# First modulation weights over 128 partitions, and Q and K of token tiles 4 to 7 with the tokens stationary, in a transformer block with dilated local attention

## The chip, the core and the metric

The kernel runs on one core of a Trainium2 chip. A core has five engines that work side by side: TensorE (PE in the profile, its weight loads apart as PEld), VectorE (DVE), ScalarE (ACT), GpSimd (POOL) and SyncE (SP), which here only issues DMAs. Each engine takes its instructions in program order and waits on semaphores for the others. PE multiplies a stationary operand (loaded first, at most 128x128) with a moving one, and its sums go to PSUM, from where ACT or DVE copy them out; all other data lies in SBUF, 128 partitions wide. A DMA can also turn a tile (rows to columns) on its way from SBUF to SBUF; in the profile that is DMA_TRANSPOSE.

The metric is the device time of one execution in microseconds (us), the median of several runs.

## What is computed

```python
mod = (silu(c) @ w_mod).reshape(1, 6, 1, 448)        # c is 1 x 448, w_mod 448 x 2688
sa, ca, ga, sb, cb, gb = six rows of mod
h = layernorm(x) * (1 + ca) + sa                     # x is 1 x 2048 x 448
x = x + ga * attention(h, wqkv, wo)
h = layernorm(x) * (1 + cb) + sb
x = x + gb * mlp(h)          # layernorm, 448 -> 1792, tanh gelu, 1792 -> 448, with biases
```

The attention has 16 heads of 28 channels. Token s attends to the 8 tokens s, s-2, ..., s-14, as far as they exist. Inputs and the output are bf16.

## The kernel before

**Tokens.** Because of the step of 2, even and odd tokens never meet in the attention. A *token tile* p (0 to 7) holds 128 even and 128 odd tokens; the index `s` or `n` (0 or 1) tells them apart. 448 channels are three full rows of 128 and a half row of 64 (`KT = 4`, `KS = 64`).

**The head of the kernel.** `c` is laid out as columns by four small matmuls (`c_cols`), silu is made of it, and `silu_bc` holds it for use in matmuls. The first two sixths of `w_mod` (sa and ca) are loaded into `wm_st` as 112 partitions by 4 rows (`MW = 112`, `KM = 4`), in two DMAs of 588 and 196 KB. `mod_cols` (L396, 40 matmuls) turns them into the columns `mod_col`, which scale and shift the normalized tokens (`affine`, L475 and L477) into `hT`, channels on partitions. The other four sixths go through `wmod2` and `mods` (L597) to `mod_bc` by way of a small buffer in HBM (L604, L606).

**Q and K** (`front_qk`). The weights are staged in `wqk_st` and `wqr_st`, and `spread` (L418 to L427) copies them to `Wqk` and `Wqr` with 32 columns for each head's 28, so that a group of four heads fills 128 partitions. These 128 columns are the stationary operand, and up to 512 tokens move: the sum stands in PSUM with channels on partitions, as the attention wants it, and ACT copies it to `qT` or `kT`. Tiles 0 and 1 go alone, then 2 and 3, 4 and 5, 6 and 7 as pairs. A pair costs, for Q and K together, four groups of 6 matmuls with 128 rows (L526) and 4 with 64 rows (L532, two of which run side by side).

**Attention** in 9 batches of 114 positions: V from `hT` (`v0` to `v8`; batches 5 to 8 first copy overlapping windows of `hT` into `hw`, L646), logits (`lt`, L695), exp, mask, the sum of the weights (`pd`) and the weighted V (`po`, L728), whose product with the inverse sum (`omul`, L745) is written over `qT`. `out_proj` (`wo0` to `wo7`, L760) is followed by two layer norms on DVE, with the power -1/2 on POOL (L447); their result `zy` is turned to `yT` by DMA (L791). The first layer norm of tiles 4 to 7 is turned by DMA as well (`zT`, L500); that of tiles 0 to 3 by PE.

**MLP** by pairs of tiles: `w1` (L526 and L532 with `yT`), gelu on ACT, `w2` (L840), the residual and the store. It comes in three phases between which ACT changes its function table, and the later attention batches run between `w2` matmuls.

**What sets the order.** All work is first recorded as numbered tasks with an engine each. `emit` then issues them in the order of a table, `ORDER`: `n` is a task's number, `n:A`, `n:D`, `n:P` an engine other than its first choice (ACT, DVE, POOL), `n:R` a variant of a PE task with the half rows first, and `n+k@m` puts k *fillers* ahead, matmuls on zeros of 128x256 (L369) which keep PE at work while it waits. `SLOTS` picks for each temporary tile one of the buffers of its kind (`ROOM`); PSUM has four (`P`). So each engine's sequence is fixed; nothing is decided while it runs. SP issues all loads, turns and stores in one sequence, but for one small load by ACT.

Of the kernel before, what the change touches and what calls it, by code (L numbers as in the profile page):

```python
# [9 lines left out]
FP32 = mybir.dt.float32  # L10
BF16 = mybir.dt.bfloat16
ACT = mybir.ActivationFunctionType
ALU = mybir.AluOpType
# [4 lines left out]
KM, MW = 4, 112  # L18
# [5 lines left out]
LEAD = 8  # L24
PLACE = (0, 2, 1, 3)
WT = LEAD + SL + 8
# [10 lines left out]
UNITS = [[0], [1], [2, 3], [4, 5], [6, 7]]  # L37
PHASES = [(range(0, 5), [0]), (range(5, 7), [1]), (range(7, 9), [2, 3])]
ROOM = {"P": 4, "et": 2, "den": 2, "zy": 4, "h2": 3, "yT": 3, "hm": 2, "vb": 3, "xp": 3, "hw": 2}
# [10 lines left out]
]  # L50
ORDER = """
0 13 3 15 1 9 14 7 16 6 17 11 10 12 8 18 19 5 2 52+9@52 4 20 60 21 58 53 22 61 54 59 55 23 62 56 63 57 64 24 68+10@68
65 66 67 25 69 70 26 76 71 27 77 72 73 74 28 75 84+10@84 78 85 29 81 86 82:A 30 98 90+3@90 83:A 31 91 80:A 96 92 93
94:R 99 79 32 97 128 100 87 120 101 88:R 95 33 102 103 164 34 121 89 129 130 35 118 104:A 36 189 105 165 131 119 166
190 132 122 108 133 37 109:A 169 106 107:A 187 123 170 179 209+5@209 38 177 167 124 125 113 134 210 39 168 114:R 135
178 126 180 136:A 254 40 127 181 115 244 182 137 255 188 110 246 138:A 41 141 111:R 191 171 42 139:A 245 192 150 256
43 112 140 44 172 183 151 311 193 45 174 257 247 184 46 258 248 185 152 175 194 214 312:D 259 211 146 186 215 195 261
212 260 216 142:R 148 262:D 196 213 249 147 144:D 263 250 143:R 251 149 252:D 153 47 217 145 48 173 49 218 200 219 50
197 276 198 51 199:A 176 253 220 205 418 154 277 221 156 278 207 281 159 206 155 279 161 282 162 222 280 208 283 266:A
157 284 285 223 286 201 158 287 224 163 202:R 203 225 288 264 316 267 204 313 226 289 265 317 227 160 314 228 318 269  # L60
290 229 454:A 315 348 271 351 291 273 293 352 292 230 294 231 349 295 353 272:R 275 232 350 268 233 274 296 236 234
116 298 319 270 297 320 117 235 299 354 321 346 237 300 356 238 301 239 419 322 303 302 240 347 304 241 305 323 455:R
306 527:A 242:D 307 357 243 308 355 309:D 324 381 358 310 456 359 325 420 563:A 328 528 360 329 397:R 326 529 363 361
382 364 327 362 398 330 365 331 399 366 332 367 368 387:R 333 386 369 383 334 384 370 385 335 371 400 404 392 373 391
336 401 389 374 372 337 388 338 402 375 390 339 340 341 460 394 411 403 395 396 342 343 393 413 376 344:A 417 345 378
377 414 379 461 380 457 421 462 458 424 412 425 459 407 422 415 426 416 408 423 428 427 463 429 405 465 406 430 466
564 431 490 409 464 506 565 410 467 496:R 507 508 468 497 499 500 432 469 498 470 491 472 433 471 473 434 474 436 475
501:R 435 494 437 438 477 492 476 439 495 493 478 440 569 441 503 479 520 504 442 505 480 509 512 482 502 522 481 511
526 483 484 523 443 570 513 446 533 444 566 485 534 447 530 445 521 448 571 531 486 514 535 567 532 568 536 524 449
573 538 515 510 525 539 450 537 487 451 572 488:A 540 516 452 489 574 575 453 541 599 576 517 542 577 518 543 519 615  # L70
578 545 600:R 579 616 581 617 546 580 582 544 583 547 584 548 605 603 585 604 550 586 602 549 587 601 551 588 610:R
609 552 607 589 618 619 555 608 591 621 606 590 553 620 556 625 592 554 611 593 557 613 558 614 623 622 612 559 626
560 594 561:A 562 631 595 596 597:D 598 629 630 624 635 627 628 650:R 638 639 637 632 636 652 640 653 654 633 651 657
634 655 656 645:R 641 644 643 642 664 648 649 646 660 647 665 658 666 667 659 668 669 661 670 671 672 662 673 663 674
675
# [76 lines left out]
def kernel(  # L152
# [65 lines left out]
    c_row = cst.tile([1, D], BF16, name="c_row")  # L218
    one1 = cst.tile([1, 128], BF16, name="one1")
    zys = [cst.tile([128, NS, DP], BF16, name=f"zy{i}") for i in range(ROOM["zy"])]  # L220
    e_c = cst.tile([MW, KM], FP32, name="e_c")
    silu_bf = cst.tile([MW, KM], BF16, name="silu_bf")
    silu_bc = cst.tile([MW, KM, HP], BF16, name="silu_bc")
# [8 lines left out]
    wm_st = sb("hm", [MW, KM, 2 * D], BF16, "wm_st")  # L232
    wqk_st = sb("hm", [128, KT - 1, 2 * D + HP - DH], BF16, "wqk_st")
    wqr_st = sb("yT", [128, 2 * D + HP - DH], BF16, "wqr_st")
    wmod2 = sb("hm", [MW, KM, 4 * D], BF16, "wmod2")
# [81 lines left out]
    def load_rest(a):  # L317
        load(lambda a=a: nc.sync.dma_start(out=wqr_st.t[KS * a:KS * a + KS, :], in_=A_wqkv[(KT - 1) * 128:D, 0:2 * D + HP - DH]),
             0.36, [f"wr{a}"], bufs=[wqr_st])
# [11 lines left out]
    add("ACT", 0.4, lambda: nc.scalar.dma_start(out=c_row[:], in_=c), writes=["c"], late=1.8, name="load c")  # L331
    tbl0 = add("ACT", 1.28, lambda: nc.scalar.preload_act_table_set(EXP_SET), name="tbl")
    load_x(0, 1)
    KP = (range(KM - 1), range(KM - 1, KM))
# [13 lines left out]
    for k in range(KM):  # L348
        load(lambda k=k: nc.sync.dma_start(out=wmod2.t[:, k, :], in_=w_mod[k * MW:(k + 1) * MW, 2 * D:6 * D]), 1.5, [f"wmod2{k}"],
             bufs=[wmod2])  # L350
# [23 lines left out]
    def c_cols():  # L374
        for k in range(KM):
            nc.tensor.matmul(psc.t[0:MW, 0, 128 * k:128 * k + 128], lhsT=c_row[0:1, k * MW:(k + 1) * MW], rhs=one1[:], start=True, stop=True)

    add("PE", 0.45, c_cols, mode="32x128", reads=["c", "one1", "warm_w"], bufs=[psc], fills=[psc], name="c_cols")
    add("ACT", 0.12, lambda: nc.scalar.activation(out=e_c[:], in_=psc.t[0:MW, 0, 0:128 * KM:128], func=ACT.Exp, scale=-1.0), bufs=[psc],
# [3 lines left out]
    add("DVE", 0.08, lambda: nc.vector.tensor_tensor(out=silu_bf[:], in0=e_c[:], in1=psc.t[0:MW, 0, 0:128 * KM:128], op=ALU.mult),  # L383
        reads=["e_c"], bufs=[psc], writes=["silu"], name="silu")
    add("ACT", 0.3, lambda: nc.scalar.copy(out=silu_bc[:], in_=silu_bf[:].unsqueeze(2).to_broadcast([MW, KM, HP])),
# [3 lines left out]
    def mod_cols(i):  # L389
        for j in range(KT):  # L390
            for v in range(2):
                for kt in KP[i]:

                    for a in range(2 if j == KT - 1 else 1):
                        m = KS if j == KT - 1 else 128
                        nc.tensor.matmul(pscol[i].t[KS * a:KS * a + m, 0, (v * KT + j) * HP:(v * KT + j + 1) * HP],  # L396
                                         lhsT=wm_st.t[:, kt, v * D + j * 128:v * D + j * 128 + m], rhs=silu_bc[:, kt, :],
                                         start=(kt == KP[i][0]), stop=(kt == KP[i][-1]),
                                         tile_position=(0, KS * a) if j == KT - 1 else None)

    head_tr, head_norm = ([], []), ([], [])

    def modulation():
        for i in range(2):
            add("PE", (0.8, 0.32)[i], lambda i=i: mod_cols(i), reads=["silu_bc", f"wm{i}"], bufs=[pscol[i], wm_st], fills=[pscol[i]], mode="F>128x64",
                name="mod_cols", instr=(60, 20)[i], after=head_tr[i])
            part = add_col if i == 0 else mod_col
            add("DVE", 0.08, lambda i=i, part=part: nc.vector.tensor_tensor(out=mod_col[:], in0=pscol[i].t[:, 0, 0:2 * KT * HP:HP], in1=part[:], op=ALU.add),
                bufs=[pscol[i]], reads=["add_col"], writes=["sca"], after=head_norm[i], name="sca")
# [73 lines left out]
    def front_ln(u, on_act, dma=False):  # L483
# [5 lines left out]
        for q, p in enumerate(u):  # L489
# [20 lines left out]
            if p == 0:  # L510
                head_norm[0].append(P.tasks[-1])
            tr_task = add("PE", 0.45, tr, reads=["ident"] + zk, bufs=[*ptr, z], writes=[(ptr[0], q)], instr=16, name=f"tr{p}")
            if p == 0:
                head_tr[1].append(tr_task)
                modulation()
# [396 lines left out]
```

## Time and profile before

| | |
|---|---|
| runs | 176.03, 176.88 and 177.47 us, median 176.88 |
| span of the profiled execution, first to last instruction | 174.2 us |
| median less span | 2.7 us |
| granted TensorE clock, mean | 1.000 |
| PE matmuls | 2152 |
| HBM read and written | 9.81 MB and 1.84 MB |

The page names no time of the profiled execution beside its span. A span is measured from the first instruction to the last, so a constant part before and after is missing in it; the table gives what it comes to against the median.

In the profile's lists a group reads: line, engine, operation, tiles (out<-in), shapes, count, then busy us and mean ns of one, then the idle time just ahead of it and who ended it. For matmuls the mean is the time of one through the pipeline; the next one starts earlier, so the cost of a row of them is read from the chain of waits, where consecutive pieces are given from start to start.

### The profile page before, as it was taken

How to read it: one execution, taken by the hardware profiler on the slowest of the kernel's cores; microseconds unless marked ns; L12 is line 12 of the kernel's file. 1: busy time of each engine (PE TensorE's matmuls, PEld its weight loads, DVE VectorE, ACT ScalarE, POOL GpSimd, SP SyncE). 2: the span in 40 equal slices, each digit the busy share in tenths (PEclk: the TensorE clock that was granted, in tenths of full speed). 3: DMA queues.
4: the chain of work that ended last, by engine and by line, in shares of the span. 5: the costliest groups of instructions: out<-in, count | busy, mean ns of one | idle time of the engine just before them, and what ended most of it. 6: DMA issues, size and time to landing. Idle time of an engine off the chain costs nothing.

```text
span 174.2 us, 4984 instructions
## 1 busy us (share of the span) xinstructions
PE 167.4 (96%) x2152; PEld 84.9 (49%) x2152; DVE 115.1 (66%) x289; ACT 108.1 (62%) x147; POOL 42.5 (24%) x60
## 2 busy tenths in 40 slices
PE   7799999998999999999999999999899999999993
PEld 4585564353454444444555353554444455344562
DVE  6477998569999989796254259998597950220103
ACT  3156989497889798478939644976625840166400
POOL 6002134003013320367000004655003840053000
PEclk9999999999999999999999999999999999999999
DMA  5999999989000014000610100001910028100002
GB/s 146 294 307 297 237 212 338 221 235 229 6 0 4 4 30 93 4 0 0 124 56 0 56 0 0 4 0 56 124 53 0 2 45 79 55 36 17 0 30 79
DMA packets 20708, 15.12 MB, mean 87 GB/s; under 512 B 13705, under 2 KB 19726, under 8 KB 20686
## 3 DMA queue, kind: packets, MB, share of 16 engines
q1 hardware_dynamic: 20684, 14.80, 36.2%
q8 instruction: 17, 0.28, 0.7%
q14 instruction: 5, 0.04, 0.1%
q10 hardware_dynamic: 2, 0.00, 0.0%
HBM read 9.81 MB, written 1.84 MB: 67 GB/s over the span
## 4 chain that ended last, share of the span: by engine, by line
PE 83%; DVE 9%; DMA 3%; issue 1%; ACT 1%; SPq 0%
PE p L840 21%; PE p L526 18%; PE pq L526 12%; PE pw L760 6%; PE pv L663 5%; PE p L532 3%; DMA wm_st<-in_w_mod_dram 3%; PE po L728 3%; PE pv L526 3%; PE pq L532 3%; PE lt L695 3%; DVE stt L431 3%; DVE h L776 2%; DVE h L451 2%; PE pq L369 1%
## 5 line engine op out<-in xcount | busy, mean ns | idle before, releaser
L821 ACT ACTIVATE hm<-p,b_col 128x512 bf16<-128x512 f32 x56 | 34.1, 689 | 30.7 <-PE p L532 25.2
L840 PE MATMUL p<-w_s,hm 128*128 128x448 bf16 (+1 forms) x238 | 44.4, 342 | 0.6 <-issue 0.6
L526 PE MATMUL p<-yT,w_s 128*128 128x512 bf16 x168 | 38.5, 380 | 0.0
L447 POOL TENSOR_TENSOR rs_all<-tv_all,neg_half 128x2 f32<-128x2 f32 x22 | 18.2, 832 | 79.8 <-DVE tv_all L445 79.8
L840 PEld LDWEIGHTS <-hm 128*128 128x128 bf16 x238 | 22.7, 98 | 19.7 <-issue 1.4
L526 PEld LDWEIGHTS <-w_s 128*128 128x128 bf16 x168 | 15.7, 98 | 20.9 <-issue 3.4
L846 DVE TENSOR_TENSOR x_all<-p,x1p 128x896 bf16<-128x896 f32 (+2 forms) x10 | 9.0, 904 | 24.9 <-PE p L840 24.8
L526 PE MATMUL pq<-hT,Wqk 128*128 128x512 bf16 (+1 forms) x108 | 22.2, 345 | 0.0
L431 DVE BATCH_NORM_STATS2 stt<-x_all 128x6 f32<-128x448 bf16 x32 | 18.4, 610 | 0.2
L798 POOL TENSOR_TENSOR x1p<-x_all,gbb_bc 128x448 f32<-128x448 bf16 x16 | 17.6, 1122 | 0.0
L702 ACT ACTIVATE et<-lt 128x928 bf16<-128x928 f32 x18 | 16.0, 946 | 1.3 <-PE lt L695 1.3
L745 DVE TENSOR_TENSOR qT<-po,den 128x912 bf16<-128x912 f32 x9 | 9.9, 1103 | 7.0 <-ACT den L739 5.2
L526 PEld LDWEIGHTS <-Wqk 128*128 128x128 bf16 x108 | 9.4, 98 | 9.7 <-issue 2.9
L708 DVE TENSOR_TENSOR et<-et,mask 128x928 bf16<-128x928 bf16 x18 | 11.2, 644 | 3.6 <-ACT et L702 3.6
L760 PE MATMUL pw<-wo_s,qT 128*128 128x448 bf16 x64 | 13.1, 353 | 0.0
L767 DVE TENSOR_TENSOR x_all<-pw,x_all 128x896 bf16<-128x896 f32 x8 | 8.7, 1084 | 6.6 <-PE pw L760 6.6
L586 ACT CAST kT<-pq 128x1024 bf16<-128x1024 f32 x8 | 8.1, 1015 | 5.3 <-PE pq L532 3.3
L737 ACT ACTIVATE den<-pd 128x928 f32<-128x928 f32 x9 | 8.3, 946 | 4.6 <-PE pd L717 4.6
L776 DVE TENSOR_TENSOR h<-h,mod_bc 128x896 bf16<-128x896 bf16 x16 | 10.2, 672 | 0.0
L739 ACT ACTIVATE den<-den,den_bias 128x928 f32<-128x928 f32 x9 | 9.5, 1072 | 0.1
L431 DVE BATCH_NORM_STATS2 stt<-h 128x6 f32<-128x448 bf16 x16 | 9.1, 614 | 0.1
L760 PEld LDWEIGHTS <-qT 128*128 128x128 bf16 x64 | 6.0, 98 | 5.7 <-issue 0.2
(102 smaller groups left out, 184.0 us busy)
## 6 DMA issues: line engine op xcount, KB each, us to landing
wmod<-in_w_mod_dram SPq DMA_DIRECT2D x4, 392.0 KB, 10.5
w_s<-in_B_w_dram SPq DMA_DIRECT2D x7, 224.0 KB, 5.7
out_dram<-x_all SPq DMA_DIRECT2D x7, 224.0 KB, 2.6
x_all<-in_A_x_dram SPq DMA_DIRECT2D x3, 448.0 KB, 5.5
w_s<-in_B_w_dram SPq DMA_DIRECT2D x3, 448.0 KB, 4.8
wqk_st<-in_A_wqkv_dram SPq DMA_DIRECT2D x3, 225.0 KB
wm_st<-in_w_mod_dram SPq DMA_DIRECT2D x1, 588.0 KB, 5.8
x_all<-in_A_x_dram SPq DMA_DIRECT2D x2, 224.0 KB
```

The source lines that it names most:

```text
L431: add("DVE", 0.53, lambda: nc.vector.bn_stats(out=stt[:, w, b, :], in_=src()), reads=reads, bufs=bufs, after=early if w == b == 0 else (), ...
L447: add("POOL", 0.55 + 0.17 * n, lambda: nc.gpsimd.tensor_tensor(out=r, in0=tv, in1=neg_half[:, 0:n], op=ALU.pow), reads=[f"tv{w}_{b0}", "ne ...
L526: nc.tensor.matmul(out(), lhsT=lhs(kt, slice(0, 128)), rhs=rhs(kt, slice(0, 128)), start=first and kt == 0, stop=not first and kt == KT - 2)
L532: nc.tensor.matmul(out(), lhsT=lhs(KT - 1, rows), rhs=rhs(KT - 1, rows), start=first, stop=not first, tile_position=(rows.start, 0))
L702: exps.append(add("ACT", 0.83, lambda half=half, lt=lt: nc.scalar.activation(out=et.t[:, 2 * half:2 * half + 2].rearrange("p r m c -> p r ...
L708: nc.vector.tensor_tensor(out=ev, in0=ev, in1=mask[:], op=ALU.mult)
L745: nc.vector.tensor_tensor(out=qT[:, :, LEAD + q00:LEAD + q00 + 2 * WQ], in0=po.t[:, :, 0:NS * 4 * WQ].rearrange("p j (m c) -> p m j c", c=WQ),
L760: nc.tensor.matmul(pw.t[:, s, 0:D], lhsT=qT[:, NS * PLACE[ft] + s, LEAD + 128 * p:LEAD + 128 * p + 128], rhs=wo_s[:, ft, :], start=(ft == ...
L776: add("DVE", 0.55, lambda vec=vec, op=op: nc.vector.tensor_tensor(out=h2.t[:], in0=h2.t[:], in1=vec.unsqueeze(1).to_broadcast([128, NS, D] ...
L798: add("POOL", 1.0, lambda n=n: nc.gpsimd.tensor_tensor(out=x1p.t[:, n, :], in0=xn(p, n), in1=gbb2_bc[:], op=ALU.add), reads=[f"x{p}", "gbb ...
L821: gelus.append(add("ACT", 0.585, lambda f=f, a=a, p1=p1s[g]: nc.scalar.activation(out=hm.t[:, f].rearrange("p n c -> p (n c)"), in_=p1.t[: ...
L840: nc.tensor.matmul(p2.t[:, n, 0:c1 - c0], lhsT=hm.t[:, f, n, q * 128:(q + 1) * 128], rhs=w2_s[:, f, c0:c1], start=(f == parts[0][0]), stop ...
```

## The change

**1. First modulation weights.** `wm_st` is 128 partitions by 3 rows (one DMA of 672 KB), the last 64 channels go to `wm_r` by two DMAs of 64 partitions and 56 KB each. `c_row` is loaded by two DMAs of ACT, the second for the half row. `mod_cols` has 24 matmuls with 128 rows and 8 with 64 rows, and the columns of the half row come from `wm_d`, which four new DVE copies (`twice`) fill. Both sets of `mod_cols` now stand ahead of the first turn `tr0`, where the second stood behind it. `wmod2` too has 128 partitions, by 3 rows and a half row.

**2. Q and K of tiles 4 to 7** (`natural_qk`). The 128 tokens of one parity are the stationary operand, and the 448 weight columns move, straight out of `wqk_st` and `wqr_st`, for each tile, half (1 is K, 0 is Q) and parity: 8 tasks of 6 matmuls with 128 rows and 2 with 64 rows. The sum has tokens on partitions. ACT (or DVE) copies 28 of every 32 columns into a `zy` buffer, of which there are five now instead of four, and a DMA_TRANSPOSE of SP writes it to `qT` or `kT`: 8 new ones (`tk4`, `tq4` and so on).

**3. Layout.** Block m of `qT` and `kT` is now `KT * s + ft` (parity, then head group) instead of `NS * PLACE[ft] + s`, in the logits, in `po` and in `out_proj`; `LEAD` grows from 8 to 16 columns.

**4. Engines and order.** `spread` and the window copies may go to POOL. `ORDER` and `SLOTS` are new throughout. Fillers: 36 instead of 37.

```diff
-    wm_st = sb("hm", [MW, KM, 2 * D], BF16, "wm_st")
+    wm_st = sb("hm", [128, 2 * KT - 2, D], BF16, "wm_st")
+    wm_r = sb("yT", [128, D], BF16, "wm_r")
+    wm_d = sb("h2", [128, 2 * KT - 1, 2 * KS], BF16, "wm_d")
...
-    for i, ks in enumerate(KP):
-        load(lambda ks=ks: nc.sync.dma_start(out=wm_st.t[:, ks[0]:ks[-1] + 1, :],
-                                             in_=w_mod[ks[0] * MW:(ks[-1] + 1) * MW, 0:2 * D].rearrange("(k p) n -> p k n", p=MW)),
-             (2.25, 1.25)[i], [f"wm{i}"], bufs=[wm_st])
+    load(lambda: nc.sync.dma_start(out=wm_st.t[:].rearrange("p (k v) n -> p k (v n)", v=2), in_=rows128(w_mod[0:(KT - 1) * 128, 0:2 * D])),
+         2.1, ["wm0"], bufs=[wm_st])
+    for v in range(2):
+        load(lambda v=v: nc.sync.dma_start(out=wm_r.t[KS * v:KS * v + KS, :], in_=w_mod[(KT - 1) * 128:D, v * D:v * D + D]),
+             0.25, [f"wmr{v}"], bufs=[wm_r])
...
+    def natural_qk(p):
+        c0 = LEAD + 128 * p
+        for half in (1, 0):
+            pq = psum("pq")
+
+            def item(s, half=half, pq=pq):
+                return (lambda: pq.t[:, s, 0:D], lambda kt, rows: hT[rows, NS * kt + s, c0:c0 + 128],
+                        lambda kt, rows: (wqk_st.t[:, kt] if kt < KT - 1 else wqr_st.t[rows])[:, half * D:half * D + D])
+
+            summed([item(s) for s in range(NS)], 0.1895, [f"wqk{k}" for k in range(KT - 1)] + ["wr0", "wr1"] + [f"h{kt}_{p}" for kt in range(KT)],
+                   [pq, wqk_st, wqr_st], [pq], f"qk{p}_{half}n")
+            st = fixed("zy", zys)
+            src = lambda pq=pq: pq.t[:, :, 0:D].rearrange("p s (h d) -> p s h d", h=H)
+            to = lambda st=st: st.t[:].rearrange("p s (h e) -> p s h e", h=H)[:, :, :, 0:DH]
+            add("ACT", 0.80, lambda to=to, src=src: nc.scalar.copy(out=to(), in_=src()), bufs=[pq, st], writes=[(st, 0)], name="evac_qk",
+                alt={"DVE": (1.0, lambda to=to, src=src: nc.vector.tensor_copy(out=to(), in_=src()))})
+            dst = (kT if half else qT)[:, :, c0:c0 + 128]
+            add("SP", 1.25, lambda st=st, dst=dst: nc.sync.dma_start_transpose(out=dst, in_=st.t[:].rearrange("p s e -> p (s e)")),
+                reads=[(st, 0), "pads"], bufs=[st], writes=[f"{'qk'[half]}{ft}_{p}" for ft in range(4)], xfer=1.3, name=f"t{'qk'[half]}{p}")
...
-                alt={"ACT": (0.93, lambda: windows(nc.scalar.copy))})
+                alt={"ACT": (0.93, lambda: windows(nc.scalar.copy)), "POOL": (1.1, lambda: windows(nc.gpsimd.tensor_copy))})
```

The parts of the new sequences that matter, as the built programs have them (numbers behind a name are token tiles for qk, t, z, y, wo and x, batches for v, lt, pd and po):

```
PE before: ... pd1 po0 po1 v2 qk4(K, first) lt2 qk4(K, second) wo0 pd2 po2 qk4(Q) lt3 wo1 qk6(Q, second) lt4
               qk6(K) qk6(Q, first) b1 pd3 po3 pd4 v4 v5 v6 po4 wo2 wo3 v7 | w1 of tiles 0 and 1 ...
PE after:  c_cols, 9 fillers, mod_cols, 2 fillers, mod_cols, tr0, 9 fillers, first Q and K with 3 fillers among them ...
           v2 pd1 qk2(Q) K4 lt2, 5 fillers, v1 Q4 pd2 po1 lt3 po2 lt3 wo0 wo1 Q5 lt4 v3 v4 pd3 Q7 Q6 pd4 po4 po3
               K5 v6 v5 K7 wo3 wo2 K6 | w1 of tiles 0 and 1, with v7 among it ...
SP after:  loads up to b1, zT4 zT5, mod_hbm, mod_bc, b2, two loads of w1, zT7 zT6 tk4 tq4, rest of w1, four loads of w2,
           tq5 tq7, two loads of w2, tq6 yT1 yT0, last load of w2, tk6 tk7 tk5 yT3 yT2, stores and turns as before
POOL after: ident, mask1, six spreads, powers and tails of tiles 2 and 3, mask, powers of 4 to 7, windows of batch 6,
           powers of the second layer norms of tiles 0 and 1, windows of batch 7 ...
DVE after: the seven scalings of w2 (L617) stand behind the second layer norms of tiles 0 and 1; before, they stood ahead.
```

More of the change, by code (lines that the diff above doesn't have):

```diff
@@ L374, in c_cols @@
     def c_cols():
[L375 to L379, printed above, removed]
+        for k in range(KT):
+            nc.tensor.matmul(psc.t[:, 0, 128 * k:128 * k + 128], lhsT=c_row[0:1, k * 128:(k + 1) * 128], rhs=one1[:], start=True, stop=True)
+    add("PE", 0.45, c_cols, mode="32x128", reads=["c", "c1", "one1", "warm_w"], bufs=[psc], fills=[psc], name="c_cols")
+    add("ACT", 0.12, lambda: nc.scalar.activation(out=e_c[:], in_=psc.t[:, 0, 0:128 * KT:128], func=ACT.Exp, scale=-1.0), bufs=[psc],
         writes=["e_c"], after=[tbl0], name="e_c")
@@ L419, in spread @@
                 bufs=[wqk_st], writes=[f"W{half}{k}" for k in ks], port=True, name="spread",
-                alt=half and {"ACT": (0.13 + 0.43 * n, lambda dst=dst, src=src: nc.scalar.copy(out=dst(), in_=src()))})
+                alt={"ACT": (0.13 + 0.43 * n, lambda dst=dst, src=src: nc.scalar.copy(out=dst(), in_=src())),
+                     "POOL": (0.1 + 0.5 * n, lambda dst=dst, src=src: nc.gpsimd.tensor_copy(out=dst(), in_=src()))})
         for a in range(2):
@@ L426, in spread @@
                 bufs=[wqr_st], writes=[f"Wr{half}{a}"], port=True, name="spread r",
[L427 removed]
+                alt={"ACT": (0.33, lambda rows=rows, src=src: nc.scalar.copy(out=Wqr[rows, half], in_=src())),
+                     "POOL": (0.4, lambda rows=rows, src=src: nc.gpsimd.tensor_copy(out=Wqr[rows, half], in_=src()))})
     def stats(src, w, b, reads, bufs=()):
```

169 lines of the change are left out of this document (91 added, 78 removed), and 11 rows, old and new, of the table SLOTS.

## The prediction

> **What bounds the kernel now.** I read the page first, for who is busy, and the chain that ended last.
>
> ```profile
> span 174.2 us, 4984 instructions
> ...
> PE 167.4 (96%) x2152; PEld 84.9 (49%) x2152; DVE 115.1 (66%) x289; ACT 108.1 (62%) x147; POOL 42.5 (24%) x60
> ...
> PE 83%; DVE 9%; DMA 3%; issue 1%; ACT 1%; SPq 0%
> ```
>
> PE is busy for 167.4 of 174.2 us and makes up 83% of the chain. A busy PE need not be at its peak, so I went on to the chain of waits in order of time (start, length, what), which gives the cost of each piece from start to start and the places where PE stood.
>
> ```profile
> 1.26 5.85 DMA wm_st<-in_w_mod_dram
> 7.16 1.10 PE ps_col L396 x24
> ...
> 9.60 2.04 PE pq L369 x10
> ...
> 12.29 0.33 PE pq L369 x3
> ...
> 17.07 0.91 ACT vb L678
> ...
> 40.27 0.86 issue
> ```
>
> The chain begins with a load: the first modulation weights land at 7.11, and until then PE has nothing but fillers. From 7.16 on nearly all of it is PE. The exceptions named here, 0.91 for a copy of V and 0.86 of issue, are small. So the time is the head, plus the sum of PE's work, plus a few stalls, plus a short tail (last addition and store) that the change leaves as it is. DVE and ACT have a third of the span free on average, but not in the stretch ahead of the first `w1` (columns: stretch, length, then busy us and count of PE, PEld, DVE, ACT, POOL, then clock, DMA share, GB/s):
>
> ```profile
> 48.00:54.00 6.00, 6.00 (x153) 3.10 (x151) 5.84 (x13) 5.15 (x7) 0.69 (x1) 1.00 0.00 0
> 54.00:60.00 6.00, 6.00 (x108) 2.67 (x108) 5.97 (x19) 5.02 (x7) 2.63 (x1) 1.00 0.01 3
> ```
>
> There DVE works 5.84 and 5.97 of 6 us and ACT 5.15 and 5.02, while the DMA engines rest (share 0.00 and 0.01). Whoever wants `w1` to start sooner must relieve DVE there.
>
> **Q and K of tiles 4 to 7: PE work.** The chain shows a whole pair of tiles in the old form in one stretch, behind one batch's logits, and the windowed V of two batches, which has the very shape of the new form (6 matmuls of 128 rows and 2 of 64 rows over 448 columns each):
>
> ```profile
> 27.93 0.63 PE lt L695 x62
> 28.56 1.40 PE pq L526 x6
> 29.96 0.54 PE pq L532 x4
> 30.50 2.70 PE pq L526 x12
> 33.20 0.54 PE pq L532 x4
> 33.73 1.40 PE pq L526 x6
> ...
> 61.33 1.24 PE pv L526 x6
> 62.58 0.48 PE pv L532 x4
> 63.06 1.24 PE pv L526 x6
> ```
>
> Old: 1.40 + 0.54 + 2.70 + 0.54 + 1.40 = 6.58 a pair, 13.16 for two. New: (1.24 + 0.48 + 1.24) / 2 = 1.48 a task, 8 x 1.48 = 11.84. The difference, **1.3 us**, is the padding of 28 to 32 columns that is no longer multiplied. It lies on PE, so it counts in full where PE doesn't wait. The copies out of PSUM are now eight of 896 columns, the size of `vb` at 17.07 (0.91), and beside other work of ACT and DVE.
>
> **The head.** Loads bound it. Before, 224 KB of x and 588 KB of weights come first; after it 224 and 672, then 112, so the bytes up to the last modulation weight are the same. The rates differ by layout:
>
> ```profile
> 4.00:6.00 2.00, 2.00 (x10) 1.23 (x9) 1.69 (x8) 0.86 (x4) 0.00 (x0) 1.00 1.06 262
> ...
> 12.00:14.00 2.00, 2.00 (x21) 1.43 (x20) 2.00 (x7) 0.74 (x3) 0.00 (x0) 1.00 1.09 329
> ```
>
> While the 112-partition tile moves, 262 GB/s; later, with 128-partition tiles and the DMA engines no fuller (1.06 and 1.09), 329. The 1,008 KB (1.03 million bytes) at 262 GB/s take 3.9 us, at 329 take 3.1: an estimated **0.8 us** sooner. That is as much as PE can use, nearly, since the fillers ahead of the modulation stay:
>
> ```profile
> 3.89 2.31 PE L369 MATMUL ps_col<-warm_w 128*128 128x256 bf16 x10
> ```
>
> They end at 6.20; with 9 instead of 10 at 6.0, so the first real matmul comes at most 1.2 us sooner than 7.16. The bounds are 0 and 1.2, and I take the 0.8 of the rates. Behind it the work is level: 32 modulation matmuls for 40, but 2 + 9 fillers where 10 stood.
>
> A rule of the Trainium skill speaks against this gain. *DMA: Bandwidth & Descriptors*, section "Why a DMA increments its semaphore by 16 and not by 1", has a DMA use the largest number of queues up to 16 that divides its rows, so 112 rows would use all 16, as 128 do; by that alone the rate would stay, the 0.8 us would fall away, and the time would be 174.6, inside the forecast's own range. The rows of 262 against 329 speak against its being the whole story.
>
> Fillers run at two speeds: 2.04 / 10 = 0.20 us each at 9.60, 0.33 / 3 = 0.11 at 12.29, with the same shape. PE doubles its pace at about 11.2 us. If the new head, which closes the idle time ahead of the modulation, brings that forward, its 9 late fillers shorten by up to 0.9 us; if not, the first matmuls of Q and K, which now stand some 0.8 us earlier, run at half pace and give 0.4 of it back. I take neither.
>
> **Stalls and order.** The new order does not repeat the places of 0.91 and 0.86, 1.8 us. It has places of its own, priced next; I let them take 0.8 and count a net **1.0 us**, between bounds of +1.8 and -5.5.
>
> First place: the turns. Eight more stand in SP's sequence.
>
> ```profile
> wmod<-in_w_mod_dram SPq DMA_DIRECT2D x4, 392.0 KB, 10.5
> ...
> zT<-zy SPq DMA_TRANSPOSE x4, 5.0
> ```
>
> Q of tile 4 is the tight one. PE has between its last matmul and `lt4` two `wo` (1.62 each, row below), Q5 (1.48) and a batch of logits (0.63): 5.4, and pd2, po1 and po2 on top. The copy (0.91) and the turn (5.0) need 5.9. So it lands just in time, if nothing is queued ahead. Ahead of it are zT7, zT6, tk4 and two loads of `w1`, which SP issues as soon as their tiles are there; queued behind it on SP are the rest of `w1` and the first of `w2`, which nobody needs before the `w1` block. K5, K6 and K7 are turned during the first `w1` block and used after it.
>
> Second place: DVE ahead of `w1`. This is the span from `wo1` to `w1`, and the work that leaves DVE there:
>
> ```profile
> 49.73 1.62 PE pw L760 x8
> ...
> 69.69 3.99 PE p L526 x18
> ```
>
> ```profile
> L617 DVE TENSOR_TENSOR w_s<-w_s,mod_bc 128x896 bf16<-128x896 bf16 x7 | 4.2, 614 | 0.0
> ```
>
> Before, 69.69 - 49.73 = 20.0 us, in which the DVE chain of tiles 0 and 1 must run and `yT` land. After, PE has between the start of `wo1` and `w1`: three `wo` (4.9), six Q or K tasks (8.9), four V (6.0, at 1.48 or a little more), a batch of logits (0.6) and the pd and po of two batches: a little over 20 as well. DVE has the 4.2 us of `w2` scalings (L617) out of its way, so the chain fits, with 1 or 2 us to spare or to lack. That PE gets there some 5 us earlier is no gain in itself: V of batch 7 and the scalings come later instead.
>
> **Sum.** 0.8 + 1.3 + 1.0 = 3.1 us; span 174.2 - 3.1 = 171.1. The median lies 176.88 - 174.2 = 2.7 over the span, the same after: **173.8 us**.
>
> **Rivals.**
>
> *The relief is eaten by POOL and the tight chains (same).* The window copies of batches 6 and 7 move from ACT to POOL; that of batch 6 stands ahead of the powers (L447) on which the layer norms of tiles 0 and 1 wait. POOL's small power shows what company does:
>
> ```profile
> 50.94 0.69 POOL L447 TENSOR_TENSOR rs_all<-tv_all,neg_half 128x2 f32<-128x2 f32 x1 [10.28 <-DVE tv_all L445]
> 55.17 2.63 POOL L447 TENSOR_TENSOR rs_all<-tv_all,neg_half 128x2 f32<-128x2 f32 x1 [3.54 <-DVE tv_all L445]
> ```
>
> The same instruction took 0.69 alone and 2.63 while DVE was full. Two such delays of 1.9 in that chain make `w1` 2 us late after what slack there is: 175.8. Against it: only one of the two shown is long. Chance 0.16. A rule of the Trainium skill says the same: *SBUF — State Buffer*, section "SBUF: two separate sides", has DVE and GpSimd lock a shared pair of ports for a whole instruction, while the other blocks fully. The row of 2.63 agrees.
>
> *The turns come late (slower).* If Q4's turn waits behind loads as `wmod` did, it lands after 10.5 instead of 5.0 and `lt4` stands 5.5 - 0.5 = 5 us with all of PE behind it; 173.8 + 5 = 178.8. It is slower by over 1% from a landing 5.4 us late on (0.5 of slack, 3.1 of gain, 1.8 of the bound below), which the 5.5 just exceeds. For it: the row of `wmod` shows what a full queue does. Against it: from 48 to 60 us the DMA engines rest before, and of weights only two loads of `w1` are queued ahead of Q4. Chance 0.15.
>
> *Everything fits and PE doubles its pace early.* The gain in the head is 1.2 + 0.9, the stalls give 1.8: 1.3 + 2.1 + 1.8 = 5.2, so 171.7. Chance 0.12. The Trainium skill's *TensorE: Matmul & The Clock Gate*, Part 1, puts the step after about 3.4 us of sustained work, by which a head without the pause ahead of 7.16 would see it well before 11 us. The trace agrees so far: the step came some 4 us after that pause.
>
> **How the numbers follow.** My forecast has 0.57, with its own range of 172.6 to 175.0. 1% of 176.88 is 1.8 us, about what a measurement of this kernel can tell from no change: faster is below 175.1, slower above 178.7. Faster: 0.57 + 0.12 = 0.69. The POOL rival falls within 1%. Of the late turns I put the greater part, 0.13, over 178.7 and the rest within: same 0.18, slower 0.13. The range runs from 171.2, with most of the fast case inside, to 178.0, which takes in the POOL case and leaves out most of the late turns: about 0.2 outside.
>
> **What would show it.** `wm_st` landing at about 6 us and the first L396 matmul below 6.5; the pieces of Q and K on a line of their own or L526 with about 1.48 a task; TensorE's matmul count lower by 9; no wait of `lt` for a DMA `qT<-zy`; the first L526 matmul of `w1` near 64 us instead of 69.69. Wrong would be: a stall of `lt` or of `w1` of several us, POOL's windows far over 1 us, or a first matmul still near 7.

## The result, and the profile after

| | before | after |
|---|---|---|
| median (lowest to highest) of four runs | 176.87 (176.03 to 177.47) | 188.21 (185.47 to 188.45) |
| span of the profiled execution | 174.2 | 186.8 |
| PE busy, matmuls | 167.4, 2152 | 169.7, 2143 |

The ratio, which leaves out disturbed runs and so can differ from the quotient of the medians, is 1.0574, with a 95% interval of 1.0488 to 1.0659: the kernel is slower by about 6%, where 173.8 us (171.2 to 178.0) was forecast. From the page of the kernel after:

```profile
span 186.8 us, 5005 instructions
...
PE 169.7 (91%) x2143; PEld 86.7 (46%) x2143; DVE 122.5 (66%) x287; ACT 105.7 (57%) x145; POOL 50.2 (27%) x70
...
PEclk9999999998599999999996999999999999999997
...
q8 instruction: 17, 0.28, 0.6%
```

PE stands still for 17 us now instead of 7, and it is busy 2.3 us longer for nine matmuls fewer. A slower clock goes with that: the row PEclk, all nines before, has dips at its tenth and eleventh slice (42 to 51 us) and at its 22nd (98 to 103); the 7 of the last slice lies behind PE's last matmul. The row of the instruction queue comes into play later. The waits of PE, the longest first (in total, how often, the longest):

```profile
PE p L541 <- DMA yT<-zy: 3.1, 1, 3.1
PE lt L727 <- issue: 2.8, 1, 2.8
PE pd L749 <- DVE et L740: 2.1, 2, 1.5
PE po L760 <- issue: 1.3, 1, 1.3
...
PE lt L727 <- DVE hT L489: 1.1, 1, 1.1
```

Together 10.4 us in these five rows, where the forecast had let the new order's stalls take 0.8. The chain of waits shows two of them, and what the old form of the row means:

```profile
40.70 0.40 PE po L760 x46
41.10 1.32 issue
42.42 0.26 PE po L760 x18
...
43.70 0.24 PE lt L727 x14
43.94 2.76 issue
46.70 0.47 PE lt L727 x15
47.17 5.39 PE pw L792 x16
52.56 1.14 PE pq L535 x6
53.69 0.29 PE pq L541 x2
...
68.29 3.03 PE pw L792 x16
```

"issue" is time in which the engine waited for nothing that the profile shows. Both pauses lie in the middle of a task, behind matmul 46 of 64 and 14 of 32, where nothing new is needed from another engine. Behind the longer one the two `wo` (`pw` in the chain) take 5.4 us; two others at 68.29 take 3.0. The windows give the clock and the DMA share there and behind the wait for `yT`:

```profile
36.00:42.00 6.00, 5.10 (x147) 2.79 (x147) 4.19 (x8) 4.58 (x6) 0.71 (x1) 1.00 1.09 202
42.00:48.00 6.00, 2.83 (x149) 2.07 (x150) 2.76 (x3) 2.56 (x3) 0.00 (x0) 0.74 1.20 228
48.00:54.00 6.00, 6.00 (x31) 2.47 (x32) 3.31 (x5) 2.97 (x5) 1.04 (x1) 0.69 0.62 185
...
96.00:102.00 6.00, 3.36 (x12) 1.25 (x13) 2.12 (x2) 2.91 (x4) 0.00 (x0) 0.79 0.16 44
```

The wait for `yT` has its origin here (timeline of the same kernel; in brackets the idle time and who ended it):

```profile
91.14 2.29 DVE L740 TENSOR_TENSOR et<-et,mask 128x928 bf16<-128x928 bf16 x4
91.29 2.29 POOL L477 COPY zy<-zy 128x128 bf16<-128x128 bf16 x1 [0.80 <-DVE zy L465]
```

A copy of 128 columns, the last step before the turn, took 2.29 us on GpSimd, where a copy of the same size took 0.16 on DVE (at 89.42): it ended 0.15 us behind DVE's four masks. SP issued the turn behind it, and PE stood until 98.6.

### The profile page after: what moved, and what is told of

Read it like the earlier page. It is cut to its first block, busy times and chain, and to the rows that moved or that the text cites. A ratio compares the mean times of both kernels' runs of the same rounds, so it can differ in the third digit from the quotient of the medians.

```text
span 186.8 us, 5005 instructions
## 1 busy us (share of the span) xinstructions
PE 169.7 (91%) x2143; PEld 86.7 (46%) x2143; DVE 122.5 (66%) x287; ACT 105.7 (57%) x145; POOL 50.2 (27%) x70
## 4 chain that ended last, share of the span: by engine, by line
PE 68%; issue 12%; DVE 7%; ACT 5%; DMA 3%; POOL 2%; SPq 0%; DVEq 0%; POOLq 0%
PE p L872 17%; PE p L535 15%; PE pq L535 10%; PE pw L792 6%; PE pv L695 3%; DMA wm_st<-in_w_mod_dram 3%; PE p L541 3%; PE pq L541 2%; ACT et L734 2%; PE po L760 2%; PE pv L535 2%; DVE h L808 2%; PE lt L727 2%; DVE h L465 2%; POOL zy L477 1%
## 5 line engine op out<-in xcount | busy, mean ns | idle before, releaser
L535 PE MATMUL p<-yT,w_s 128*128 128x512 bf16 x168 | 40.0, 392 | 0.0
L461 POOL TENSOR_TENSOR rs_all<-tv_all,neg_half 128x2 f32<-128x2 f32 x22 | 16.8, 781 | 80.8 <-DVE tv_all L459 74.5
L445 DVE BATCH_NORM_STATS2 stt<-x_all 128x6 f32<-128x448 bf16 x32 | 19.0, 614 | 0.9 <-DMA x_all<-in_A_x_dram 0.6
L792 PE MATMUL pw<-wo_s,qT 128*128 128x448 bf16 x64 | 15.0, 396 | 0.0
L465 DVE TENSOR_SCALAR h<-x_all,mvs,rs_all 128x448 bf16<-128x448 bf16 x16 | 9.9, 647 | 1.7 <-POOL rs_all L461 1.7
L535 PE MATMUL pq<-hT,Wqk 128*128 128x256 bf16 (+1 forms) x60 | 10.7, 317 | 0.0
L727 PE MATMUL lt<-qT,kT 28*64 28x58 bf16 x576 | 7.1, 193 | 3.9 <-issue 2.8
L541 PE MATMUL p<-yT,w_r 64*128 64x512 bf16 x56 | 7.8, 379 | 3.1 <-DMA yT<-zy 3.1
L535 PE MATMUL pq<-wqk_st,hT 128*128 128x448 bf16 x48 | 10.3, 353 | 0.0
L792 PEld LDWEIGHTS <-qT 128*128 128x128 bf16 x64 | 6.8, 108 | 7.4 <-issue 2.7
```

The source lines that it names most:

```text
L445: add("DVE", 0.53, lambda: nc.vector.bn_stats(out=stt[:, w, b, :], in_=src()), reads=reads, bufs=bufs, after=early if w == b == 0 else (), ...
L461: add("POOL", 0.55 + 0.17 * n, lambda: nc.gpsimd.tensor_tensor(out=r, in0=tv, in1=neg_half[:, 0:n], op=ALU.pow), reads=[f"tv{w}_{b0}", "ne ...
L465: add("DVE", 0.31, lambda: nc.vector.tensor_scalar(out=dst(), in0=src(), scalar1=mvs[:, w, b, 0:1], scalar2=rs_all[:, w, b:b + 1], op0=ALU ...
L535: nc.tensor.matmul(out(), lhsT=lhs(kt, slice(0, 128)), rhs=rhs(kt, slice(0, 128)), start=first and kt == 0, stop=not first and kt == KT - 2)
L541: nc.tensor.matmul(out(), lhsT=lhs(KT - 1, rows), rhs=rhs(KT - 1, rows), start=first, stop=not first, tile_position=(rows.start, 0))
L727: nc.tensor.matmul(lt.t[WK * j:WK * j + WK, r % 2, c0:c0 + WE], lhsT=kT[HP * r:HP * r + DH, m, k0:k0 + WK], rhs=qT[HP * r:HP * r + DH, m, ...
```

## The experiments

Each ratio is to runs of the kernel before that were made beside it on the same chip. e1 to e4 have such runs in common, and so have e5 to e7, e8 and e9, e10 and e11; from one of these groups to another the ratios are to be compared, not the medians.

**Which DMAs, if any?** The pauses lie where the DMA share is 1.09 and 1.20, with turns and weight loads together. The first two kernels move the loads away, ahead or behind, and the third leaves out the turning; the fourth moves the copy of 2.29 us to DVE.

```diff
e1, SP's sequence:  loads up to b1r
+                   b2, five loads of w1, four of w2
                    zT4 zT5 mod_hbm mod_bc
-                   b2, two loads of w1
                    zT7 zT6 tk4 tq4
-                   three loads of w1, four of w2
                    tq5 ...
e2, SP's sequence:  the same nine loads behind tq5, b2 where it was
e3, natural_qk:
-  nc.sync.dma_start_transpose(out=dst, in_=st.t[:].rearrange("p s e -> p (s e)"))
+  nc.sync.dma_start(out=dst, in_=st.t[:].rearrange("p s (f c) -> p (s f) c", c=128))
e4, ORDER:
-  362        (tail of tile 2's second layer norm, on GpSimd)
+  362:D
```

(The expectations call it tile 3's or leave it open; task 362 is tile 2's.)

> The kernel after, with b2, the five loads of w1 and the first four of w2 issued ahead of zT4 and zT5 instead of behind them; nothing else moves. Theory A (PE's own instructions come by DMA in 16 KB packets, and the two packets that were late, at 40.01 and 44.47, stood in a DMA system filled by weight loads and turns together): the DMA share at 36 to 48 us falls from 1.09 and 1.20 to well below 1, the pauses of 1.32 us in po1 and 2.76 us in lt3 go (each under 0.5), the granted clock of 42 to 54 us stays above 0.95, so the two wo behind it take 3.0 instead of 5.4 us; 4.1 + 2.4 = 6 to 7 us less, about 182, unless the wait for yT at 95 us grows by as much. Theory B (the eight new turns alone are the cause): the pauses stay within 1 us of 4.1 and the time stays at 186 to 188.5. Theory C (the pauses belong to the order of PE's own work and have nothing to do with DMAs): the same as B.

> The kernel after, with the five loads of w1 and the first four of w2 issued behind tq5 (at about 55 us) instead of around the turns of 37 to 44 us: between zT7 and tq5 only turns are left on the DMA engines. Theory A with the weight loads as the culprit: both pauses (1.32 and 2.76 us) go, 4 to 6 us less, 182 to 184, less what w1 loses if its weights land after 72 us. Theory A with the turns as the culprit, or theory B: a pause of 1 to 3 us is left between 40 and 47 us, with a 16 KB packet that ends 1.2 to 1.5 us before PE goes on. Theory C: both pauses stay as they are, 4.1 us together.

> The kernel after, with the eight turns of K and Q (tk, tq) replaced by DMAs of the same bytes between the same tiles that do not turn, so K and Q of tiles 4 to 7 hold wrong values: the turning is left out. Where the DMA engines are filled by the many small packets of the turns, the share at 36 to 48 us falls, the pause of 2.76 us in lt3, which lies in the two turns tk4 and tq4, goes or shrinks below 1 us, the one of 1.32, which lies behind zT7 and zT6 that still turn, may stay; 183 to 185. Where the weight loads alone fill them: both pauses stay, 186 to 188.5. Theory C: both stay as well.

> The kernel after, with one copy of 128 columns, the tail of tile 3's second layer norm ahead of its turn yT3 or yT2, on DVE instead of GpSimd. In the kernel after this copy took 2.29 us on GpSimd (91.29 to 93.58) while DVE worked on a mask, and PE then stood 3.1 us for that turn at 95.4; on DVE a copy of the same size took 0.16. Theory D (the wait at 95 us comes from this copy): the turn is issued some 2 us sooner, the wait falls from 3.1 to about 1 us, the clock behind it stays above 0.9 instead of 0.79, 2 to 3.5 us less, 184.5 to 186. Rival: the turn waits for the norms on DVE anyway, which stand behind the masks; then nothing changes.

| | median | ratio (95% interval) | pause in po1 | pause in lt3 |
|---|---|---|---|---|
| e1 | 189.61 | 1.0648 (1.055 to 1.0746) | none | 2.43 |
| e2 | 184.29 | 1.036 (1.0264 to 1.0455) | none | 2.85 |
| e3 | 186.67 | 1.0507 (1.0427 to 1.0586) | 1.04 | 2.77 |
| e4 | 181.51 | 1.023 (1.0156 to 1.0304) | 0.13 | 3.00 |

Theory A fell as it stood. The pause in po1 comes and goes, but the one in lt3 is in all four, even in e2, where from 42 to 48 us the DMA engines are half idle:

```profile
41.31 0.24 PE lt L727 x14
41.55 2.85 issue
44.40 0.43 PE lt L727 x18
```

```profile
42.00:48.00 6.00, 3.60 (x27) 1.64 (x28) 1.51 (x3) 3.76 (x6) 0.00 (x0) 0.72 0.50 41
```

Always behind matmul 14 of 32. e1 lost elsewhere what it gained: PE stood 2.4 us at 32.8 for `hT` of tiles 4 and 5, whose turns were now queued behind the loads. e4 bore theory D out and more: the wait for `yT` is gone, with the dip of the clock behind it (about 1.7 us: 6 x 0.21 from 96 to 102 us and 6 x 0.08 in the next 6, whose clock was 0.92). That makes 4.8; the rest of its 6.7 (6.1 by the ratios) is the nearly absent pause in po1 and the head, 6.06 for 6.80, which the edit doesn't touch.

**What the pauses are.** The trace records when the packets of the queue in the row `q8 instruction` moved. I counted PE's instructions (matmuls, weight loads and a few of its sequencer) up to each pause:

```
kernel   instructions of PE   packet from   to      PE goes on   after the packet's end
before        1217               38.91     39.79      41.14          1.35
before        3777              119.84    120.92     122.41          1.49
after         1217               40.01     40.97      42.42          1.45
after         1473               44.47     45.43      46.70          1.27
e1            1473               43.66     45.15      46.59          1.44
e2            1473               42.06     42.99      44.40          1.41
e3            1217               38.68     39.63      41.00          1.37
e3            1473               42.98     43.87      45.28          1.41
e4            1473               42.56     43.44      45.02          1.58
```

The counts are the same in every kernel, before too, and 1473 - 1217 = 256; the third, 0.57 us in a `w2` of the kernel before, lies ten packets further, 3777 - 1217 = 10 x 256. A packet has 16,384 bytes, 64 for each of 256 instructions. The Trainium skill, *Trainium Architecture — The Big Picture*, section "The software stack", gives an instruction 64 bytes, which agrees; that section has the streams brought to the engines when the program is loaded, where this trace shows 17 packets under way. PE goes on 1.3 to 1.6 us after a packet's end. So theory E: PE runs out of instructions. `po` and `lt` are the fastest eaters, with 128 and 64 a task in 0.64 and 0.38 us, and the new order has `pd2`, `po1`, half of `lt3`, `po2` and the other half in a row: 16 + 128 + 64 + 128 + 64 = 400 instructions. Two tests: spread these tasks (e5), and leave their order but shift the count (e6). A third looks for the same thing in the kernel before (e7).

```diff
e5 (with e4's edit), PE's sequence:
-  pd2 po1 lt3(1st) po2 lt3(2nd) wo0 wo1 Q5 lt4 v3 v4
+  pd2 po1 lt3(1st) Q5 po2 wo0 lt3(2nd) wo1 v4 lt4 v3
e6 (with e4's edit):  41 fillers ahead of v1 instead of 5, in filler():
-  nc.tensor.matmul(t.sums[0].t[:, 0, 0:256], ..., rhs=warm_w[:, 0:256], ...)
+  w = 256 if i < 9 else 16
+  nc.tensor.matmul(t.sums[0].t[:, 0, 0:w], ..., rhs=warm_w[:, 0:w], ...)
e7 (kernel before), PE's sequence:
-  lt2(1st) lt2(2nd) K4/5(2nd group) wo0
+  lt2(1st) K4/5(2nd group) lt2(2nd) wo0
```

> The kernel of the run before this one in the list of ideas (after, with the tail copy of tile 3 on DVE, 181.5 us), and in it PE's order around the pause changed: from pd2, po1, first half of lt3, po2, second half of lt3, wo0, wo1, Q5, lt4, v3, v4 to pd2, po1, first half of lt3, Q5, po2, wo0, second half of lt3, wo1, v4, lt4, v3 (Q5 takes another PSUM buffer for it). Theory E (PE runs out of instructions: a packet of 16 KB holds 256 of them, and po and lt use up 400 in 2.2 us where a packet takes 3.5 to 5 us from the point that seems to ask for it to its use): with Q5 and wo0 between them, 3.0 us of work of 16 instructions each, the pause at 41.8 to 45.0 (3.0 us) shrinks to under 0.8, the clock stays above 0.95 from 42 to 54 us and the two wo cost 3.1 together; 4 us less, 177 to 178.5. Rival (the pause belongs to the turns tk4 and tq4 that land then): the pause stays at its time, 42 to 45 us, wherever PE is, and 2 to 3 us of it are left; 180.5 to 182.

> The kernel after with the tail copy of tile 3 on DVE (181.5 us), and 36 more fillers of 16 columns each ahead of v1, 72 instructions with their weight loads. Theory E: PE runs dry at the same count of instructions from the start, 1473 in all four traces so far, so the pause moves 36 matmuls forward, out of the second half of lt3 (behind its matmul 14 of 32) into po2 (behind its matmul 42 of 64), with the count still 1473, and it lasts 2.5 to 3.5 us; the time is 181.5 and about 0.3 to 0.9 for the fillers. Rival (a wait of lt3 for something that the trace doesn't show, such as a PSUM buffer or a turn): the pause stays in the second half of lt3, behind its matmul 14.

> The kernel before, with one PE task moved: the second half of lt2 behind the second group of K of tiles 4 and 5, instead of ahead of it. Theory E: before has the same kind of pause, 0.86 us at 40.27 behind matmul 36 of lt2's 64, at 1217 instructions, which is 256 fewer than 1473, and its packet ended at 39.79, 1.35 us before PE went on. With 1.6 us of work of few instructions ahead of that point the pause goes or falls below 0.3, and the time is 0.6 to 0.9 less than before: ratio 0.995 to 0.997. Rival: the pause belongs to lt2 or to that time and stays, ratio 1.000.

e6 measured 179.87, ratio 1.0151 (1.005 to 1.0251), and its chain:

```profile
41.39 0.38 PE lt L728 x32
41.77 0.43 PE po L761 x42
42.19 1.95 issue
44.15 0.28 PE po L761 x22
44.42 0.38 PE lt L728 x32
44.80 4.81 PE pw L793 x16
```

The pause has left lt3 and stands behind matmul 42 of 64 of po2, as foretold, at the count of 1473; it was shorter (1.95) than the 2.5 to 3.5 expected, which fits a time below e4's and not above it. A wait of lt3 for a buffer or a turn would have stayed in lt3. (Of the 36 fillers added, four have 256 columns and 32 have 16.) e5 measured 178.50, ratio 1.0085 (1.0012 to 1.0158), 3.0 less than e4 by the medians and 2.6 by the ratios:

```profile
42.19 0.61 PE po L760 x64
42.80 0.00 issue
42.80 1.11 PE pw L792 x5
43.91 0.47 issue
44.38 0.74 PE pw L792 x3
45.12 0.38 PE lt L727 x32
45.49 1.63 PE pw L792 x8
```

0.47 is left of 3.00, again at 1473, and the two `wo` around it take 1.9 and 1.6 instead of 2.3 each, with no slow clock. e7 measured 0.999 (0.9919 to 1.0061), which decides nothing about the time. The pause at 1217 is gone, but PE stands 1.9 us for `qT` (a PSUM buffer that `omul` frees late) a little earlier. e9, the kernel before itself, shows this wait too, and no pause at 1217: the one or the other limits that place. (e9 has its pause at 3777, 1.25 us.)

**What is left.** e5 has waits of 1.2 us (lt1), 1.7 (pd6) and 0.5 (pd8, 0.9 with the matmuls around it) that the kernel before has not, or not so long.

```diff
e8 (e5's kernel), ORDER:
-  150:A 151:A 174 225 175 149 148    (copies of hT out of PSUM, 149 and 148 on DVE)
+  150:A 149 151:A 148 174 225 175
-  w2(tile 1, last group 1st part) pd6 w2(2nd part) pd5 po6 po5
+  w2(1st part) w2(2nd part) pd6 po6 pd5 po5
-  pd8 w2(tile 2, 1st part) w2(2nd part)
+  w2(tile 2, 1st part) pd8 w2(2nd part)
e9: the kernel before, unchanged
```

(For "tile 4" in the expectation of e8 read tile 2.)

> The kernel of e5_spread with four more moves: (a) the four copies of the first layer norm of tiles 2 and 3 out of PSUM alternate between ACT and DVE in the order ACT, DVE, ACT, DVE instead of two of ACT ahead of two of DVE, since DVE's two stood 1.53 us for ACT's two and the second half of lt1 stood 1.2 us for them; (b) the last w2 group of tile 1 ahead of pd6 instead of behind it, and po6 ahead of pd5, since pd6 stood 1.7 us for a mask; (c) pd8 behind the first w2 group of tile 4, since it stood 0.9 us for a mask. If these waits are what is left of the difference (1.2 + 1.7 + 0.9 = 3.8 us, of which about 1 us of (b) is given back to the turn of tile 2 that lands then): 175 to 176, ratio to before 0.988 to 0.995, pauses of at most 0.5 us each at the three places. Rival: DVE, which is the longer part of the chain from 47 to 60 us in e5_spread, sets the end; then PE stands elsewhere for it and the time stays at 177.5 to 178.5.

> The kernel before, once more, for the start of its first modulation matmul alone. In its profile this stood at 7.16, in the run with lt2 moved, whose head is the same, at 6.12; the new head gave 6.80, 6.04, 5.82, 5.98, 6.06, 6.00 and 5.63. If the new layout saves 0.8 us of load, this start lies near 6.7 or above; if the load takes the same in both layouts and only varies from execution to execution, it lies between 5.6 and 6.3.

e8: 177.04, ratio 0.9993 (0.9952 to 1.0033), 1.0 to 2.0 short of what was expected. The waits went (all `pd` together 0.7, lt1 none), but a pause of 0.6 is left at 1473, and one of 0.7 came back in po1 at 1217: its packet moved from 37.71 to 38.59, and PE, which had stopped at 39.31, went on at 39.96. And I had left out the tail. The last addition in the chain of the kernel before, and in the timelines of the kernel after and of e8:

```profile
171.31 0.39 DVE x_all L846
...
182.54 0.39 DVE L878 TENSOR_TENSOR x_all<-p,x1p 128x224 bf16<-128x224 f32 x1 [0.88 <-PE p L872]
...
167.71 4.76 SPq L882 DMA_DIRECT2D out_dram<-x_all  x7
...
170.80 0.39 DVE L878 TENSOR_TENSOR x_all<-p,x1p 128x224 bf16<-128x224 f32 x1 [0.88 <-PE p L872]
```

In e8 the last addition ends at 171.19, the last of seven stores is issued by 172.47, and the span ends at 175.5, 4.3 after the addition. In the kernel before that distance is 2.5, in the kernel after 3.9. In the new sequence of SP the store of tile 7's first half stands ahead of those of tiles 3, 0 and 4, which were finished long before.

e9: the first modulation matmul stands at 6.00, below 6.3, so the first weights of the old layout were there as early in that execution as those of the new one in others; see below.

```diff
e10 (e8's kernel), the stores in SP's sequence, by tile:
-  1 ... 2 ... 5 7(1st) 3 0 6 4 7(2nd) 7(3rd)
+  1 0 ... 2 ... 5 3 4 7(1st) 6 7(2nd) 7(3rd)
e11 (e10's kernel): five loads of w1 and four of w2 behind tq5, as in e2
e12 (e11's kernel): the eight turns replaced as in e3
```

> The kernel of e8_tidy with the stores of the output put in SP's sequence in the order in which their additions end. In the kernel after and all those made of it SP stands at one store (23.4 us in e8_tidy) whose addition ends late, with stores of long finished tiles behind it; the last seven go out between 167.7 and 172.5, the last of them 1.3 us after its addition ended (171.19), and the span ends 4.3 us after that addition, where in the kernel before it ends 2.5 us after it. If the order of the stores is the cause: the last store is issued within 0.5 us of its addition, the span ends 2.5 to 3.0 us after it, 1.2 to 1.8 us less than e8_tidy, 175.2 to 175.9, ratio to before 0.990 to 0.994. Rival: the end of the span is set by the landing of the last store whatever is queued ahead of it; then 177.0 and 0.999.

> The kernel of e10_stores, and in it the five loads of w1 and the first four of w2 behind tq5, as in e2_loads_late. Theory E with DMAs: the packet of instructions that PE needs at its 1217th was asked for at about 33 us and started at 37.7 in e8_tidy, 35.9 in e2_loads_late; with fewer packets ahead of it it starts 1 to 2 us sooner and the pause of 0.85 us in po1 at 1217 goes; the one of 0.93 at 1473 shrinks below 0.6. 0.5 to 1.2 us less than e10_stores, 174.3 to 175.2, unless the weights of w1 or w2 then land late (a wait of w1 for a DMA at about 65 us). Rival: the packets are late whatever stands ahead of them; the two pauses stay and the time is that of e10_stores within 0.4.

> The kernel of e11_stores_loads with the eight turns of K and Q replaced by DMAs of the same bytes between the same tiles that do not turn, so K and Q of tiles 4 to 7 hold wrong values: the turning is left out. If the turns are hidden (they land in time and no longer hold up instructions): 174.05 within 0.6, ratio to before 0.985 to 0.992. If their packets of 256 bytes still hold up PE's instructions or delay other transfers: the rest of the pause at 1473 (0.64) and the wait ahead of pd6 shrink, 172.5 to 173.4, ratio below 0.982.

(The expectations of e11 and e12 name pauses of 0.85, 0.93 and 0.64 us; by the chain of PE's matmuls they are 0.65 and 0.58 in e8 and 0.29 in e11.)

| | median | ratio (95% interval) | pause at 1217 | at 1473 |
|---|---|---|---|---|
| e10 | 175.61 | 0.9971 (0.9927 to 1.0015) | 1.0 | 0.6 |
| e11 | 174.05 | 0.9882 (0.9817 to 0.9946) | none | 0.3 |
| e12 | 174.32 | 0.9883 (0.9833 to 0.9933) | none | none |

e10, timeline of its end: four stores where e8 has seven, and the last is issued by 171.56, 0.36 behind the last addition; the span ends at 173.9. The time is as expected, 1.4 us less than e8's; the ratio, 0.9971, is above the 0.990 to 0.994 expected, and its interval overlaps that of e8. So the gain is shown by the trace, 4.3 to 2.7 us behind the last addition, and not by the ratios.

```profile
167.71 3.85 SPq L882 DMA_DIRECT2D out_dram<-x_all  x4
...
170.81 0.39 DVE L878 TENSOR_TENSOR x_all<-p,x1p 128x224 bf16<-128x224 f32 x1 [0.88 <-PE p L872]
```

e11: the packet before 1217 starts at 34.65 instead of 37.56 in e10, and the pause in po1 is gone. So the load on the DMA engines does matter to the instructions; in the order of e2 the same move took away one pause and left the other. This kernel beats both, the kernel before by 1.2%; its page:

```profile
span 172.9 us, 5007 instructions
...
PE 166.3 (96%) x2143; PEld 85.1 (49%) x2143; DVE 123.2 (71%) x288; ACT 105.3 (61%) x145; POOL 47.3 (27%) x69
...
PEclk9999999999999999999999999999999999999999
```

e12: without the turning the ratio is the same. The eight turns cost nothing that intervals of 0.6% could show.

## Why the prediction was wrong, step by step

**The step that failed** is "Stalls and order": "I let them take 0.8 and count a net 1.0 us". The new order's places took 10.4 us of waiting (the five rows above), and the slow clock behind two of them 2.4 (two `wo`) and 1.7 more; 14.5 instead of 0.8. With the tail (1.4) and the head (0.4) that is 15.5 of the 15.7 us between the forecast span, 171.1, and 186.8. The lower bound of -5.5 was drawn for a late turn of Q of tile 4, one mechanism, and none of the five rows is that. The row that would have warned was quoted: "40.27 0.86 issue". I called it small and counted it as removed with the old order, without asking what it was. It was PE out of instructions, and the new sequence, quoted in the section on the change, has `po1`, `lt3`, `po2` and `lt3` in a row. e6 shows the mechanism and e5 its cure. Of the 14.5 us, PE out of instructions accounts for 6.5, with the clock behind it; the copy on GpSimd, which the forecast didn't price, for 4.8 (e4), and the waits of `pd` and lt1 for DVE for 3.2.

**The tail** "that the change leaves as it is" was not left: the span ends 3.9 us behind the last addition instead of 2.5, 1.4 more, and e10's order of the stores takes this back to 2.7. The new order of the stores was in SP's sequence too, which I had read only as far as the turns.

**The two tight places.** The turns, the first, were not tight: no `lt` waits for a turn of Q or K in any trace, and e12 shows them free. The rival of late turns thus had the right direction and the wrong cause. The second, DVE ahead of `w1`, was seen rightly: with the pauses gone the first `w1` starts at 65.4 in e11, for "near 64" in the forecast and 72.8 in the kernel after, and the chain of e11 there is DVE's.

**Q and K** were right: 1.14 + 0.29 = 1.43 a task in the rows above, up to 1.54 with a half row first, for 1.48; nine matmuls fewer.

**The head** was mis-sized, 0.8 for about nothing (7.16 to 6.80 between the two profiles, 0.4 less than forecast). The timeline of e7, with the old head:

```profile
3.89 2.31 PE L369 MATMUL ps_col<-warm_w 128*128 128x256 bf16 x10
6.12 1.09 PE L396 MATMUL ps_col<-silu_bc,wm_st 112*128 112x32 bf16 x30
...
8.07 1.26 PE L369 MATMUL pq<-warm_w 128*128 128x256 bf16 x10
```

There the weights are in place when the ten fillers end, and the first modulation matmul follows them at 6.12; in e9 at 6.00. The 7.16 of the profile of before was a late execution of the same load. The new head gave 5.63 to 6.80. The Trainium skill's rule (*DMA: Bandwidth & Descriptors*, section "Why a DMA increments its semaphore by 16 and not by 1") spreads 112 rows over as many DMA engines as 128, by which alone the gain falls away. So it came out for the first product, though the windows of 2 to 6 us still show 250 to 284 GB/s in three executions of the old layout and 294 to 328 in those of the new, which that rule leaves open. The doubled pace at 8 us (1.26 for ten fillers) is in the old head too, so it was no effect of the change.

**GpSimd.** The window copies were harmless, 1.04 us. The mechanism of that rival showed at another place, the tail copy of 2.29 us during DVE's masks, where the profile of before had shown 2.63 for 0.69. The Trainium skill's rule on the shared ports (*SBUF — State Buffer*, section "SBUF: two separate sides") fits both rows; that the copy stayed out through four masks and not one is this trace's own. I had looked at the powers and the windows on GpSimd and not at the copies that stand last before a turn.

Two thirds of what the forecast summed up was there to be had, but with another order of the same work: e11's ratio of 0.9882 is 2.1 us of the 3.1.

## What to carry to other kernels

A pause that no engine explains, in the middle of a row of matmuls, is to be counted in instructions before it is called small: if it falls at the same count in two versions, PE is waiting for its own code, and tasks of many tiny matmuls have to be spread among tasks of few long ones. When an order is replaced as a whole, every sequence is read to its end, stores and one-line copies too: here a copy of 128 columns cost about 5 us and the order of the stores 1.4. One profile of before is one execution: a term that rests on one late load in it (7.16) needs a second look.

## What the runs showed of the hardware

PE's instructions come in packets of 256 during the run. Every pause of PE over 0.2 us that the traces put down to "issue", 19 in all, stands behind 1217, 1473 or 3777 instructions. PE went on 1.3 to 1.6 us after the packet's end, and even with the DMA engines half idle (e2) the packet started 0.5 us after PE had stopped.

The granted clock fell after pauses far shorter than what the Trainium skill, *TensorE: Matmul & The Clock Gate*, Part 1, gives as an idle window, about 3.4 us: 1.95 us in e6 and 2.4 to 3.1 in the others, all beside `po` and `lt`, were followed by a slow clock, with pairs of `wo` at 4.6 to 5.4 us instead of 3.0 to 3.3. Pauses of 2.4 us in e1 (at 32.8) and 1.9 in e7 and e9, between rows of long matmuls, were not.

Part of this can be read from the clock in the traces. In each of them it changes only at times that lie a multiple of 3.41 us apart (in the kernel after: down to half at 44.88, up at 51.71, down at 99.50, up at 102.91). That agrees with a window that runs freely, which the same part of the Trainium skill's page describes. Counted by these stretches of 3.41 us, the full clock fell behind every stretch in which PE stood for 1.95 us or more, and behind none with 1.52 or less; the pause of e1 at 32.8 lay in two stretches, with 1.0 and 1.4 us of standing. From 1.81 to 1.92 both occur: the clock fell where the rest of the stretch was `po` and `lt` (1.81 in e3, 1.89 in the kernel after) and not where it was long matmuls (1.82 in e7, 1.92 in e9). That thin matmuls count as little work for the clock would fit; no run here tests it.
